# Issuing the stores of x's high part and of the partial output from ScalarE instead of SyncE

## The chip, the cores and the metric

The kernel runs on one core of a Trainium2 chip. The metric is the device time of one execution in microseconds (us). A core has TensorE (PE, matmuls), VectorE (DVE), ScalarE (ACT), GpSimd (POOL) and SyncE (SP); each runs its own instruction stream in order, and they wait for one another on semaphores. In the kernel before, every DMA is issued from SP's stream.

## The reference

Attention over 4 batches and 8 heads of 576 positions and 64 features, then a gated feed-forward block over the 2304 rows that it makes:

```python
scores = scale * np.matmul(q, k.transpose(0, 1, 3, 2))      # causal, softmax over keys
local = np.matmul(a, v)
mem_out = einsum(q_p, M_prev) / (einsum(q_p, z_prev) + 1e-6)  # q_p = phi(q)
x = g * mem_out + (1 - g) * local                            # rows: 2304 x 512
h = x @ w_in                                                 # 512 x 2048
g = h * np.tanh(np.log1p(np.exp(h)))
out = g @ w_out                                              # 2048 x 512
```

## The kernel before

**Attention.** Sixteen pairs of heads (`for p in range(NP)`) go through `scores` (matmuls, the row minimum on DVE at line 374, the exponential on ACT at line 381), `norm` (POOL at lines 87 and 93), `transp` (transposes, copied out of PSUM by DVE and ACT) and `av`. `av` leaves a pair's 128 columns of x as two parts: `xo`, the high part, cast by ACT out of PSUM (line 481, recorded at the helper's line 110), and `xl`, the rest, made by DVE behind it. `put` (line 484) stores both to the DRAM buffers `xs`: `xo` at line 486, `xl` at line 487. A pair has two casts to `xo`, 320 and 256 columns wide; the store follows the second.

**Feed-forward, first part.** Matmuls with w_in and w_out run on numbers split into high and low parts. The weights come as 512 KB pieces `raw` (line 152, two buffers), and `narrow` turns each into a high and a low part: `wa` on ACT (line 91), `ws` on DVE (line 156), joined on DVE (line 162), a mask on DVE (line 165), the last reading of `raw` on DVE (line 172, after which the buffer can be loaded again), the high part by ACT (line 110) and the low part by DVE (line 87). The first 6 of 16 columns of blocks (`KA`) are converted during attention, and while attention goes on `slot_a` multiplies blocks of 512 rows of x by them (line 233). `out_a` sums their share of the output in PSUM (`acc`, line 246), ACT copies it to the one buffer `ob` (line 251, recorded at line 110), and line 253 stores it to the DRAM buffer `part`. There are 18 such stores, one for each 128 rows.

**Feed-forward, second part.** `tail` first merges what is left of the first part with the conversion of seven more columns, then runs the other 10 columns over all rows (lines 566 and 583), reading x again from `xs` (line 205), and adds `part`, read back at line 581, before the output is stored at line 590.

**What sets the order.** The program is written as lists of steps; a scheduler with its own estimate of every instruction's time then orders each engine's stream, with priorities by stage (`OFF`). A stream is fixed before the run. Each DMA's completion is counted on one of eight semaphores, DMAHW0 to DMAHW7, that are handed out in turn over all DMAs; a DMA waits in its issuing stream until the one before it on the same semaphore has landed.

Of the kernel before, what the change touches and what calls it, by code (L numbers as in the profile page):

```python
# [49 lines left out]
def f32(ap):  # L50
    return ap.bitcast(F32)
# [25 lines left out]
def attention_moe_kernel(ctx: ExitStack, tc: tile.TileContext, f_src, qn, vn, zz, beta, w_in, w_out, out):  # L77
    nc = tc.nc
# [7 lines left out]
    def tt(name, **kw):  # L86
        engines[ENG[name]].tensor_tensor(**kw)  # L87
# [15 lines left out]
    def queued(ins, chain):  # L103
        if chain:
            order_after(ins, before[0])
        before[0] = ins

    def copy(which, o, i):
        if which == "a":
            nc.scalar.copy(out=o, in_=i)  # L110
        elif which == "v":
            nc.vector.tensor_copy(out=o, in_=i)  # L112
        else:
            nc.gpsimd.tensor_scalar(out=o, in0=i, scalar1=1.0, scalar2=1.0, op0=ALU.mult, op1=ALU.mult)
# [13 lines left out]
    xs = [dram.tile([128, 2, NC, S], F32, name=f"xs{b}") for b in range(B)]  # L128
    part = dram.tile([NT, DM], F32, name="part")
# [110 lines left out]
    def out_a(j, t):  # L240
        pool, tag = (("a", "acc"), ("h", "h"))[t % 2]
        acc = pool_of[pool].tile([128, DM], F32, tag=tag, name="acc")
        for f in range(KA):
            g = T[j, f]["g"]
            for y, z in ((0, 0), (1, 0), (0, 1)):
                nc.tensor.matmul(  # L246
                    acc[:], g[:, y, 128 * t:128 * t + 128], wo[z, f],
                    start=(f == 0 and y == z), stop=(f == KA - 1 and z == 1),
                )
        o = cp.tile([128, DM], F32, tag="ob", name="ob", bufs=1)  # L250
        copy("a", o[:], acc[:])
        r0 = BLOCKS[j][0] + 128 * t
        nc.sync.dma_start(out=part[r0:r0 + 128, :], in_=o[:])

    def steps_a(j):
        def first():
            X[j] = load_x(*BLOCKS[j])

        return ([first] + [lambda f=f: slot_a(j, f) for f in range(KA)]
                + [lambda t=t: out_a(j, t) for t in range(BLOCKS[j][1] // 128)])  # L260
# [3 lines left out]
    def attention():  # L264
# [194 lines left out]
        def av(p):  # L459
            d = pr[p]  # L460
            at = [hd[2 * p + e]["at"] for e in range(2)]

            def mms(j):
                if j == 0:
                    d["xo"] = tp.tile([128, S], F32R, tag="xo", name="xo", bufs=2)
                    d["xl"] = tp.tile([128, S], F32, tag="xl", name="xl", bufs=2)
                q0, ops = AVJ[j]
                n = ops[0][2]
                ps = g_["v", j] = ps_v.tile([128, n], F32, tag="v", name="vps")
                last = len(ops) - 1  # L470
                for k, (t, a, b, gi, c) in enumerate(ops):
                    for e in (1, 0):
                        queued(nc.tensor.matmul(  # L473
                            ps[64 * e:64 * e + 64, a:b], d["v"][:, t, e], at[e][gi][:, c:c + b - a],
                            start=(k == 0), stop=(k == last),
                        ), k or e == 0)

            def cp(j):
                q0, n = AVJ[j][0], AVJ[j][1][0][2]
                xo = d["xo"][:, q0:q0 + n]  # L480
                copy("a", xo, g_["v", j][:])
                tt("xlo", out=d["xl"][:, q0:q0 + n], in0=g_["v", j][:], in1=f32(xo), op=ALU.subtract)

            def put():
                b, c = divmod(p, 4)
                nc.sync.dma_start(out=xs[b][:, 0, c, :], in_=f32(d["xo"][:]))
                nc.sync.dma_start(out=xs[b][:, 1, c, :], in_=d["xl"][:])

            g_ = {}
            ops = []  # L490
            for j in range(2):
                ops += [lambda j=j: mms(j), lambda j=j: cp(j)]
            return ops + [put]
# [6 lines left out]
            out=mask[:, 448:576], in_=mask[:, 448:576], pattern=[[-1, 128]], compare_op=ALU.is_ge,  # L500
# [169 lines left out]
```

## Time and profile before

| | |
|---|---|
| median of 3 runs | 655.2 us (653.29 to 656.19) |
| the profiled execution's own time | 654.77 us |
| its span, first to last instruction | 653.0 us |
| PE, DVE, ACT, POOL busy | 597.0, 336.8, 300.7, 169.1 us |
| mean granted TensorE clock | 0.973 of full speed |
| DMA issues of line 486, 487, 253 | 16, 16, 18, all from SP |

Attention ends at about 336 us. From there to about 420 us the first part's rest and the weight conversion run together; from 420 us on PE works without pause. A busy time is a sum over the span and says nothing by itself about what is waited for; for that the waits, the chain of work that ended last and the stretches by stage are read.

### The profile page before, as it was taken

Reading aid. Unit: us, or ns where it says so; the run is one execution under the profiler, and the core shown is the slowest. Engines: PE = TensorE matmul, PEld = TensorE weight load, DVE = VectorE, ACT = ScalarE, POOL = GpSimd, SP = SyncE. Lnnn points to the kernel's source line nnn. Section 1 sums busy time; section 2 is a strip of 40 time slices with the busy share of each in tenths; the row PEclk is TensorE's granted clock in tenths of the full one; section 3 lists DMA queues with packets and bytes.
Section 4 is the critical chain, followed back from the end, with each engine's and each line's share of the span. In section 5 each row is a group of like instructions: output and inputs, shape, how many; then the busy total and the mean of one; then the engine's idle time right before and its main releaser. Section 6 shows DMA issues by size and latency. Waiting matters only on the chain.

```text
span 653.0 us, 9308 instructions
## 1 busy us (share of the span) xinstructions
PE 597.0 (91%) x3200; PEld 454.9 (70%) x3200; DVE 336.8 (52%) x903; ACT 300.7 (46%) x694; POOL 169.1 (26%) x260
## 2 busy tenths in 40 slices
PE   3477968889989999999998979999999999999997
PEld 2254635656655766767776878888888888888886
DVE  4989897765588654573338887920311211121121
ACT  3677655866567675566325455621222222222221
POOL 3697886464166714443000000000000000000000
PEclk9979986899999999999999989999999999999999
DMA  6345674324275226421257765304302220430220
GB/s 229 104 144 182 189 262 150 133 61 144 76 235 168 98 62 176 166 73 58 91 176 235 261 206 176 121 1 129 130 0 82 94 83 6 124 129 0 65 97 33
DMA packets 47007, 80.83 MB, mean 124 GB/s; under 512 B 7280, under 2 KB 21616, under 8 KB 46960
## 3 DMA queue, kind: packets, MB, share of 16 engines
q1 hardware_dynamic: 46960, 80.24, 38.0%
q8 instruction: 25, 0.41, 0.3%
q14 instruction: 22, 0.18, 0.1%
HBM read 61.35 MB, written 18.87 MB: 123 GB/s over the span
## 4 chain that ended last, share of the span: by engine, by line
PE 61%; DVE 13%; DMA 10%; ACT 7%; POOL 5%; issue 2%; SPq 1%; DVEq 0%; ACTq 0%; POOLq 0%
PE o L583 19%; PE h L566 19%; PE acc L246 7%; PE h L233 5%; DMA raw<-in_w_in_dram 5%; PE vps L473 5%; PE t L445 4%; DVE w L374 3%; PE s L364 3%; POOL w L93 3%; DMA raw<-in_w_out_dram 3%; DMA qn<-in_qn_dram 2%; ACT w L381 2%; ACT L217 1%; DVE ws L172 1%
## 5 line engine op out<-in xcount | busy, mean ns | idle before, releaser
L87 DVE TENSOR_TENSOR g<-u,g 128x512 fp32r<-128x512 f32 (+1 forms) x80 | 52.4, 661 | 185.6 <-ACT g L110 185.6
L566 PE MATMUL h<-xb,wi 128*128 128x512 f32 (+1 forms) x600 | 134.9, 368 | 0.0
L583 PE MATMUL o<-wo,g 128*128 128x512 f32 x540 | 133.8, 390 | 0.0
L217 ACT ACTIVATE u<-h 128x512 f32<-128x512 f32 (+1 forms) x80 | 43.5, 554 | 179.2 <-PE h L566 170.9
L566 PEld LDWEIGHTS h<-xb,wi 128*128 128x128 f32 x600 | 106.1, 188 | 19.6
L583 PEld LDWEIGHTS o<-wo,g 128*128 128x128 f32 x540 | 100.6, 188 | 20.3
L93 POOL TENSOR_SCALAR w<-w,rc 128x64 f32<-128x64 f32 (+4 forms) x160 | 95.4, 621 | 71.0 <-ACT w L381 53.3
L381 ACT ACTIVATE w<-w,mx 128x576 f32<-128x576 f32 (+4 forms) x160 | 88.3, 554 | 28.5 <-DVE mx L374 27.6
L364 PE MATMUL s<-f 64*128 64x288 f32 (+4 forms) x384 | 69.2, 472 | 31.7 <-DVE mx L374 25.4
L233 PE MATMUL h<-xb,wi 128*128 128x512 f32 (+1 forms) x360 | 88.0, 389 | 7.8 <-ACT u L217 7.8
L246 PE MATMUL acc<-wo,g 128*128 128x512 f32 x324 | 85.9, 401 | 1.4 <-ACT ob L110 0.9
L445 PE MATMUL t<-ident,w 128*128 128x128 f32 x480 | 75.5, 291 | 5.3 <-ACT at L110 3.1
L233 PEld LDWEIGHTS h<-xb,wi 128*128 128x128 f32 x360 | 64.8, 200 | 21.1 <-ACT u L217 9.6
L364 PEld LDWEIGHTS s<-f 64*128 64x128 f32 x384 | 35.4, 207 | 59.0 <-DVE mx L374 33.2
L445 PEld LDWEIGHTS t<-ident,w 128*128 128x128 f32 x480 | 55.9, 146 | 26.0 <-issue 8.7
L246 PEld LDWEIGHTS acc<-wo,g 128*128 128x128 f32 x324 | 59.4, 190 | 16.0 <-issue 2.3
L374 DVE CUSTOM_DVE_ANT_0 w<-s,mask 128x288 f32<-128x288 f32 (+4 forms) x160 | 59.6, 421 | 17.6 <-PE s L364 17.6
L473 PE MATMUL vps<-at,v 128*64 128x256 f32 (+2 forms) x512 | 61.3, 383 | 5.8 <-DVE xl L87 3.7
L473 PEld LDWEIGHTS vps<-at,v 128*64 128x64 f32 x512 | 35.6, 142 | 31.7 <-issue 6.0
L112 DVE COPY at<-t 128x448 f32<-128x448 f32 x64 | 41.5, 649 | 16.2 <-PE t L445 16.2
L110 ACT CAST g<-u 128x512 fp32r<-128x512 f32 (+1 forms) x80 | 45.5, 579 | 1.8
L110 ACT COPY at<-t 128x384 f32<-128x384 f32 x64 | 33.7, 526 | 17.6 <-PE t L445 17.4
(45 smaller groups left out, 432.1 us busy)
## 6 DMA issues: line engine op xcount, KB each, us to landing
f<-in_f_src_dram SPq DMA_DIRECT2D x32, 288.0 KB, 3.7
raw<-in_w_in_dram SPq DMA_DIRECT2D x16, 512.0 KB, 3.9
raw<-in_w_out_dram SPq DMA_DIRECT2D x16, 512.0 KB, 3.5
xb<-xs SPq DMA_DIRECT2D x24, 256.0 KB, 3.7
qn<-in_qn_dram SPq DMA_DIRECT2D x16, 320.0 KB, 3.4
v<-in_vn_dram SPq DMA_DIRECT2D x16, 320.0 KB, 3.3
xs<-xo SPq DMA_DIRECT2D x16, 288.0 KB, 3.4
xs<-xl SPq DMA_DIRECT2D x16, 288.0 KB, 3.3
```

What stands on the lines that cost most here:

```text
L87: engines[ENG[name]].tensor_tensor(**kw)
L93: engines[which].tensor_scalar(out=o, in0=i, scalar1=scale, scalar2=1.0, op0=ALU.mult, op1=ALU.mult)
L110: nc.scalar.copy(out=o, in_=i)
L233: ins = nc.tensor.matmul(ps, wi[y, f][:, c, :], x[c][:, z], start=(q == 0), stop=(q == 11))
L246: nc.tensor.matmul(acc[:], g[:, y, 128 * t:128 * t + 128], wo[z, f], start=(f == 0 and y == z), stop=(f == KA - 1 and z == 1),)
L364: nc.tensor.matmul(g["ps"][:, o:o + n], f[le, 0, q0:q0 + 128], f[le, 1, a:b], start=True, stop=True)
L374: nc.vector.tensor_tensor_reduce(out=g["w"][:, WO[m] + D + a:WO[m] + D + b], in0=g["ps"][:, o:o + n], in1=mask[:, c0:c0 + n], scale=-E_SC, ...
L381: nc.scalar.activation(out=row, in_=row, func=ACTF.Exp, scale=-1.0, bias=g["mx"][:, m:m + 1], accum_out=g["sm"][:, m:m + 1])
L445: nc.tensor.transpose(ps[:, o:o + 128], g["w"][:, c:c + 128], ident[:])
L473: queued(nc.tensor.matmul(ps[64 * e:64 * e + 64, a:b], d["v"][:, t, e], at[e][gi][:, c:c + b - a], start=(k == 0), stop=(k == last),), k o ...
L566: nc.tensor.matmul(ps[:, :n], wi[a, f][:, c, :], x[c][:, b], start=(k == 0), stop=(k == 11))
L583: nc.tensor.matmul(D_[t][:], g[:, y, 128 * t:128 * t + 128], wo[z, f], start=(f == KA and y == z), stop=(f == NF - 1 and z == 1),)
```

## The change

Two issues move from SP's stream to ACT's, the store of `xo` and the store of `ob`. The store of `xl` stays on SP, and so do all loads and the output. The scheduler makes its order anew.

```diff
         copy("a", o[:], acc[:])
         r0 = BLOCKS[j][0] + 128 * t
-        nc.sync.dma_start(out=part[r0:r0 + 128, :], in_=o[:])
+        nc.scalar.dma_start(out=part[r0:r0 + 128, :], in_=o[:])
...
                 b, c = divmod(p, 4)
-                nc.sync.dma_start(out=xs[b][:, 0, c, :], in_=f32(d["xo"][:]))
+                nc.scalar.dma_start(out=xs[b][:, 0, c, :], in_=f32(d["xo"][:]))
                 nc.sync.dma_start(out=xs[b][:, 1, c, :], in_=d["xl"][:])
```

ACT gains 34 rows and loses none; its 17 changes of activation table after the first stand in the same sequence. POOL's order is the same, and up to the end of attention SP's differs by the rows taken out, PE's not at all, and ACT's and DVE's by a few swaps of neighbours. From the end of attention on there are more swaps.

On ACT in the middle of attention, this is what stands now, with the semaphores that each row waits for (numbers behind names tell buffers apart; `phe` is the exponential of `prep`):

```order
L253 DMA part_77<-ob_1736 128x512 [waits DMAHW7_49,Activation_49]
L110 COPY at_1461<-t_1462 128x512 [waits PE_49]
L110 COPY ob_1758<-acc_1739 128x512 [waits DMAHW7_49]
L253 DMA part_77<-ob_1758 128x512 [waits DMAHW1_49,Activation_49]
L318 ACTIVATE phe_2238<-phe_2238 128x640 [waits DVE_49,Pool_49]
```

The two DMA rows are new in this stream; each waits for ACT's own copy and for an earlier DMA's semaphore.

On SP at the end of attention (about 336 to 344 us before), the difference; `raw` are weight pieces, `xb` blocks of x, `pp` the partial output read back:

```order
 L152 DMA raw<-in_w_in_dram 128x1024
-L486 DMA xs_76<-xo 128x576
+L152 DMA raw<-in_w_out_dram 128x1024
 L487 DMA xs_76<-xl 128x576
-L152 DMA raw<-in_w_out_dram 128x1024
 L205 DMA xb<-xs_76 128x320
-L253 DMA part<-ob 128x512
+L152 DMA raw<-in_w_in_dram 128x1024
 L205 DMA xb<-xs_76 128x320
-L581 DMA pp<-part 128x512
-L152 DMA raw<-in_w_in_dram 128x1024
-L581 DMA pp<-part 128x512 x3
```

Two weight loads have moved ahead: the second in front of the store of `xl`, the third in front of an x block and of the four `pp` loads.

On DVE in the conversion (about 357 to 361 us before), before the change:

```order
L165 TENSOR_SCALAR ws_3717<-wa_3716 128x512
L87 TENSOR_TENSOR wo1_7_3457<-wa_3666,ws_3667 128x512
L172 SCALAR_TENSOR_TENSOR ws_3717<-raw_3715,ws_3717 128x512
L87 TENSOR_TENSOR wa_3716<-wa_3716,wi0_8_3461 128x512
L87 TENSOR_TENSOR g_3757<-u_3756,g_3757 128x512
L156 TENSOR_SCALAR ws_3765<-raw_3763 128x512
```

And now:

```order
L87 TENSOR_TENSOR wo1_7_3457<-wa_3666,ws_3667 128x512
L165 TENSOR_SCALAR ws_3717<-wa_3716 128x512
L156 TENSOR_SCALAR ws_3765<-raw_3763 128x512
L172 SCALAR_TENSOR_TENSOR ws_3717<-raw_3715,ws_3717 128x512
L87 TENSOR_TENSOR wa_3716<-wa_3716,wi0_8_3461 128x512
L87 TENSOR_TENSOR g_3757<-u_3756,g_3757 128x512
```

Line 156 on the next piece, which waits for that piece to land, has moved in front of line 172 on the piece at hand, which frees the other `raw` buffer. The same has happened one column further on (`raw_3863` in front of the release of `raw_3811`).

On ACT at about 381 to 387 us before, the difference; `u` is the activation of the first 256 rows wide block:

```order
 L110 CAST wi_11_3482<-wa 128x512
 L110 COPY ob<-acc 128x512
 L91 ACTIVATE wa<-raw 128x512
-L217 ACTIVATE u<-h 128x256
-L110 CAST g<-u 128x256
-L110 COPY ob<-acc 128x512
+L253 DMA part<-ob 128x512
+L217 ACTIVATE u<-h 128x256
+L110 CAST g<-u 128x256
 L110 CAST wo_11_3483<-wa 128x512
```

A store now stands between `wa` and `u`, and the second copy to `ob` comes later.

## Rows read from the trace of the kernel before

**Rows 1.** The page: busy time of each engine; shares of the chain that ended last.

```profile
PE 597.0 (91%) x3200; PEld 454.9 (70%) x3200; DVE 336.8 (52%) x903; ACT 300.7 (46%) x694; POOL 169.1 (26%) x260
...
PE 61%; DVE 13%; DMA 10%; ACT 7%; POOL 5%; issue 2%; SPq 1%; DVEq 0%; ACTq 0%; POOLq 0%
```

**Rows 2.** Stretches: length, busy time (instructions) by engine, PE clock, DMA share, GB/s.

```profile
47.00:160.00 113.00, 94.52 (x573) 62.66 (x571) 90.33 (x268) 75.51 (x186) 73.28 (x97) 0.91 0.52 165
160.00:335.70 175.70, 169.97 (x1086) 120.14 (x1085) 97.27 (x323) 102.65 (x263) 66.53 (x119) 1.00 0.37 118
335.70:386.35 50.65, 44.46 (x197) 35.88 (x197) 40.61 (x74) 25.44 (x45) 0.00 (x0) 0.99 0.74 243
386.35:420.00 33.65, 33.65 (x165) 29.46 (x166) 27.66 (x55) 18.85 (x37) 0.00 (x0) 0.91 0.52 177
420.00:653.00 233.00, 229.10 (x1067) 191.69 (x1065) 45.49 (x74) 52.26 (x95) 0.00 (x0) 1.00 0.21 68
```

**Rows 3.** SP's waits, whole span: line, releaser, us in total, times, longest.

```profile
SPq L152 <- DVE ws L172: 59.5, 23, 7.3
...
SPq L253 <- ACT ob L110: 40.7, 16, 8.7
SPq L486 <- ACT xo L110: 33.1, 7, 23.1
...
SPq L487 <- DVE xl L87: 7.4, 5, 2.4
```

**Rows 4.** The chain that ended last, 342 to 387 us: start, length, what.

```profile
342.09 6.16 DMA raw<-in_w_in_dram
...
359.56 3.95 DMA raw<-in_w_in_dram
...
368.61 6.44 DMA raw<-in_w_in_dram
...
382.08 3.19 DMA raw<-in_w_out_dram
...
385.35 0.68 ACT wa L91
386.03 0.28 ACT u L217
...
386.35 2.93 PE h L233 x12
```

**Rows 5.** PE's waits from 335.7 to 420 us.

```profile
PE h L233 <- ACT u L217: 5.3, 3, 3.3
```

**Rows 6.** Issues of the two stores: ns shortest/median/longest, first and last start.

```profile
L486 SPq DMA_DIRECT2D xs<-xo x16: 319/354/413, 53.6 to 336.2; - x16
...
L253 SPq DMA_DIRECT2D part<-ob x18: 319/320/1172, 161.8 to 410.0; - x18
```

**Rows 7.** Timeline of SP, 341 to 358 us: start, length, line, what.

```profile
341.54 0.42 SPq L581 DMA_DIRECT2D pp<-part  x1
342.09 0.37 SPq L152 DMA_DIRECT2D raw<-in_w_in_dram  x1
...
351.60 5.31 SPq L253 DMA_DIRECT2D part<-ob  x2
357.34 0.33 SPq L152 DMA_DIRECT2D raw<-in_w_out_dram  x1
```

**Rows 8.** Timeline of ACT: start, length, line, what [idle before, releaser].

```profile
153.66 0.35 ACT L110 CAST xo<-vps 128x256 fp32r<-128x256 f32 x1
...
154.90 0.56 ACT L381 ACTIVATE w<-w,mx 128x320 f32<-128x320 f32 x1 [0.36 <-DVE mx L374]
...
166.49 0.74 ACT L318 ACTIVATE phe<-phe 128x640 f32<-128x640 f32 x1 [1.46 <-DVE phe L313]
```

**Rows 9.** Timeline of DVE, 356 to 361 us.

```profile
356.10 0.69 DVE L172 SCALAR_TENSOR_TENSOR ws<-raw,ws 128x512 f32<-128x512 uint32 x1
...
360.88 0.43 DVE L156 TENSOR_SCALAR ws<-raw 128x512 int32<-128x512 int32 x1
```

## The prediction

> **What bounds the kernel now.** I read the shares of the chain first: PE holds 61% of it, DVE 13%, DMA 10%, ACT 7%, and SP's own stream 1% [rows 1]. So time that SP spends issuing stores is hardly ever what the end waits for, and time that ACT spends issuing them falls on an engine with a small share. Then I split the span by stage [rows 2]. From 47 to 160 us PE is busy for 94.5 of 113.0 us, and DVE (90.3), ACT (75.5) and POOL (73.3) share what is waited for. From 160 to 335.7 PE is busy for 170.0 of 175.7: at most 5.7 us can be won. From 335.7 to 386.35 it is busy for 44.5 of 50.65, so 6.2 us are idle; PE waited 5.3 us there for `u` from ACT, once for 3.3 us [rows 5], and the chain runs through weight loads, DVE's conversion and ACT's `wa` up to 386.35, where PE takes it over [rows 4]. From 386.35 to 420 PE never pauses, at a granted clock of 0.91, and from 420 on it is busy for 229.1 of 233.0 at full clock [rows 2]. The change issues its last store at 410.0 [rows 6], so what it does must be done before 420.
>
> SP's waits come next [rows 3]. They look large: 40.7 us at line 253 for ACT's copy and 33.1 at line 486 for ACT's cast. Taking them away frees only what stands behind them, and that must be looked up case by case.
>
> **Part 1: SP loses 34 issues.** At medians of 0.354 and 0.320 us [rows 6] that is 16 x 0.354 + 18 x 0.320 = 11.4 us of SP's stream. Behind line 486 nearly always stands line 487, which waits for `xl`, made by DVE after `xo`; it keeps 7.4 us of waits of its own [rows 3] and will take over most of the 33.1. Behind line 253 stand loads that wait for their buffers: weight loads wait 59.5 us for DVE's line 172 [rows 3]. Going through the 18 stores I found one load that a store held: the pair of stores from 351.60 ends at 356.91, and the weight load behind it goes out at 357.34, though line 172 had freed its buffer at 356.79 (356.10 + 0.69) [rows 7, 9]. That is 0.5 us, beside the chain, which takes the load of 359.56. Part 1 by itself: 0.
>
> **Part 2: ACT gains 34 issues.** No row shows a DMA issued by ACT. From below the price is 0, if the issue fits under the running instruction; from above I take SP's longest issue of line 253, 1.17 us [rows 6]. I take 0.35 us, SP's medians, plus 0.1 where the store directly follows its copy and the next instruction can't overlap with it: the same kind of instruction should take as long in another stream. So ACT spends some 34 x 0.4 = 14 us more.
>
> By stage: 23 stores lie before 335.7, 9 between 335.7 and 386.35, 2 after. For each of the 23 I looked up ACT's next idle time behind it. In 17 it is 0.7 us or more, as at 166.49, where ACT sits idle for 1.46 us behind a copy to `ob` [rows 8]; these hide the issue. In 6 it is 0.34 to 0.58 us, as at 154.90 [rows 8], and in one of these two stores share one gap of 0.35. What sticks out is about 0.1 x 6 + 0.35 = 1 us of ACT; PE, busy for 97% of the stretch from 160 on, waits for ACT in few of these places. I take +0.4 us; the bounds are 0 and, at 1.17 us an issue, some 7 us sticking out, of which half on the path: +3.5.
>
> Of the 9, eight stand beside ACT's idle time while it waits for weights. The ninth stands between `wa` and `u`, where the chain passes: 385.35, 386.03, then PE at 386.35 [rows 4]. All of its 0.35 us lands there. The last 2 lie beside PE's unbroken work: 0. Part 2: +0.75 us, from 0 to +5.
>
> A store on ACT also waits for an earlier DMA's semaphore. If that DMA were still unissued in SP's stream, ACT would stand with it. I compared each store's moment with the DMA eight places earlier in the order: nearly all were issued 4 us or more before and had landed. Cost 0.
>
> **Part 3: the new order from 336 us on.** Here the loads run close together: 243 GB/s against 118 in the stretch before [rows 2]. The third weight load, issued at 342.09 behind a `pp` load, took 6.16 us; others on the chain took 3.2 to 3.95 [rows 4, 7]. With the x block and `pp` behind it instead of in front, I work out a landing about 1.6 us earlier: 416 KB less ahead at roughly 260 GB/s. The conversion then starts its next column 1.4 us earlier. But the next piece, loaded behind the four `pp`, lands when it did. Two columns later DVE's new order costs: line 156 waits for the next piece before line 172 frees the other buffer. Stepping DVE's rows through with its own durations (0.43, 0.60 to 0.70 and 0.44 us) and 3.5 to 3.95 us a load, the release that leads to the load of 359.56 comes 0.2 us later than before, that of 368.61 comes 0.8 us later, and that of 382.08 comes 1.1 us earlier, since there the new order frees first. So `wa` before 386.35 starts 1.1 us earlier: -1.1. The bounds: PE becomes the limit and the whole 6.2 us idle goes [rows 2], or the loads at the two new waiting places take 6.2 to 6.4 us, as those of 342.09 and 368.61 did [rows 4], which is 2 x 2.7 = +5.4.
>
> **The sum.** 0 + 0.75 - 1.1 = -0.35 us on the profiled execution's 654.77, its span of 653.0 and 1.8 around it: 654.4. That execution lies 0.4 under the median of 655.2, so for a median I forecast 654.8: no change that a measurement of this kernel, which tells apart about 0.5% or 3.3 us, can show.
>
> **The rivals.**
>
> *Faster: the conversion stops being the limit.* With stores on another stream, loads go out as soon as their buffers are free, and the stage from 335.7 loses most of its 6.2 us of PE idle time, some with it of the clock, which fell from full 2.4 GHz to a mean of 0.91 (1.2 GHz for part of the stretch) behind the pause before 386.35 [rows 2]; at 0.09 of 33.65 us that is up to 3 us more. I price it at 4 to 7 us: 648 to 651, say 650. For it: weight loads are on the chain seven times here, and the new order puts two ahead. Against it: only one load was held by a store, and the loads wait for line 172. The Trainium skill, Perfetto Trace Analysis, section DMA Optimizations, advises to give inputs to one issuing engine and outputs to another so that they spread more freely. By that rule this rival would be the forecast, at 650; no run here shows it yet, and SP's rows speak for a small effect, since what waits behind the stores waits for buffers.
>
> *Slower: DVE waits for a load before it frees the buffer for the next.* This is the upper bound of part 3. At two places more than before the two `raw` buffers work one after the other. While loads land in under about 4.5 us the gains elsewhere cover it; at 6 us or more the stage grows by up to 5.4 us, and since PE has no work of its own ahead, the end does too: 654.8 + 1.1 + 5.4 = 661; in the middle 659.5. For it: two loads of that stage took over 6 us. Against it: the x blocks and `pp` that slowed them have moved.
>
> *Slower: ACT is held at its stores.* At 0.8 us or more an issue the idle behind 10 or so of the 23 is used up, the stores beside `wa` in the conversion stick out too, and I get +4 to +5: 659. The Trainium skill, Perfetto Trace Analysis, section DMA Instruction — HWDGE (DVE, Sync), speaks for this: it says that a DMA's semaphore wait, its wait for the descriptor generator's lock and the issue all take place in the issuing engine's sequencer. By it an ACT store behind its own copy stops what follows until the copy is written; my 0.1 us stands for that, and a wait for the lock would come on top. No row here can show the lock.
>
> *That the stores don't leave SP* is excluded: SP's order has lost exactly those rows.
>
> **How the numbers follow.** Forecast, within noise: 0.62. Faster rival: 0.18. DVE's order: 0.12; ACT held: 0.08. Faster by over 0.5% is under 651.9, slower over 658.5, so the chances are 0.18, 0.62 and 0.20. For 8 in 10 the range takes in half of each side: down to 650.5, and up to 660.0.
>
> **What would show it.** Issues of lines 486 and 253 in ACT's stream of 0.3 to 0.4 us; SP's waits at line 487 grown to nearly the 33 us of line 486; the weight load near 342 landing in under 5 us; PE's wait for `u` near 386 shortened to 2 to 3 us; from 420 on the same pace. I am wrong about ACT if its issues take over 0.8 us or POOL and PE wait longer for line 381; about DVE if line 156 stands idle for a load for over 2 us at the two new places; about SP if weight loads go out well before they did although line 172 runs when it did.

## The result and the profile after

The changed kernel takes 659.17 us (median; 657.1 to 661.56) against 655.69 us for the kernel before on the same chip: a ratio of 1.0051, 95% interval 1.0036 to 1.0065. It is slower by about 3.5 us. The time lies in the predicted range (650.5 to 660.0), but "no change that can be measured" was wrong.

The profiled execution of the changed kernel took 660.73 us, its span is 658.9. One execution is a coarse measure here: the traces of the experiments below include a second one of each kernel, and the two of before have spans of 653.0 and 658.5. So sizes are taken from the timed ratios, and the traces are read for what is waited for.

The stretches of [rows 2], in the kernel after (length, busy time of PE, PEld, DVE, ACT, POOL with instructions, PE clock, DMA share, GB/s):

```profile
160.00:335.70 175.70, 170.28 (x1064) 120.18 (x1063) 96.97 (x323) 102.74 (x263) 67.40 (x120) 0.98 0.37 119
335.70:386.35 50.65, 46.44 (x210) 36.20 (x209) 35.94 (x65) 22.62 (x40) 0.00 (x0) 1.00 0.67 220
386.35:420.00 33.65, 28.47 (x153) 25.09 (x152) 27.69 (x54) 17.01 (x35) 0.00 (x0) 0.95 0.61 193
420.00:653.00 233.00, 233.00 (x1086) 195.18 (x1085) 48.81 (x81) 56.65 (x103) 0.00 (x0) 1.00 0.22 69
```

From 386.35 to 420 PE no longer works without pause: 28.47 us of 33.65, where before it was 33.65. In the last stretch PE is busy throughout; the 229.10 us of before mean only that its program ends inside the stretch. In this trace the last cast of attention also starts 3.0 us later than before (338.71 against 335.71 us), which is taken up with C2 below. Behind it, the conversion of the weights, up to 420 us, is where to look.

The new issues on ACT, which answer to [rows 6] (ns shortest/median/longest, first and last start), and then the SP waits that answer to [rows 3] (line, releaser, us in total, times, longest):

```profile
L253 ACTq DMA_DIRECT2D part<-ob x18: 326/326/353, 162.2 to 414.8; - x18
...
L486 ACTq DMA_DIRECT2D xs<-xo x16: 326/326/360, 53.9 to 339.1; - x16
```

```profile
SPq L152 <- DVE ws L172: 88.9, 27, 8.0
...
SPq L487 <- DVE xl L87: 50.9, 13, 23.7
```

An issue costs ACT 326 ns, and line 487 has taken over line 486's waits. Both are as predicted. The surprise is in the chain that ended last, 379 to 393 us (start, length, what), which answers to [rows 4]:

```profile
381.48 0.58 ACT ob L110
382.05 0.03 ACT wa L91
382.08 3.10 DMA part<-ob
...
385.26 0.07 ACT ob L110
385.33 0.42 issue
385.75 0.14 ACT wo L110
385.88 5.66 DMA part<-ob
...
391.62 0.07 ACT ob L110
391.69 0.41 issue
392.10 0.46 ACT wa L91
...
392.66 0.38 ACT u L217
...
393.09 2.08 PE h L233 x8
```

Two stores of the partial output stand on the chain, for 3.10 and 5.66 us. `ob` is one buffer: ACT's next copy to it waits until the store before has landed, and as ACT works in order, `wa` and `u` behind that copy wait too. PE gets `u` at 393.09, which is 54.4 us behind the last cast; before, at 386.35, 50.6 us behind it. Of what ACT and PE waited for between 335 and 425 us, these rows count:

```profile
ACT ob L110 <- DMA part<-ob: 7.5, 4, 2.6
...
PE h L233 <- ACT u L217: 6.9, 2, 5.2
```

In the trace of before ACT waited 0.5 us, once, for a part store there, and PE's longest wait for `u` was 3.3 us [rows 5]:

```profile
ACT ob L110 <- DMA part<-ob: 0.5, 1, 0.5
```

One trace is little: in the second trace of before these are 3.3 us and 4.5 us.

Why do the stores land so late? SP's weight loads after, and then SP's stream before with the same two loads and the same two stores (start, us, line, what):

```profile
382.18 0.33 SPq L152 DMA_DIRECT2D raw<-in_w_in_dram  x1
385.51 0.33 SPq L152 DMA_DIRECT2D raw<-in_w_out_dram  x1
```

```profile
376.25 0.32 SPq L253 DMA_DIRECT2D part<-ob  x1
377.69 0.33 SPq L152 DMA_DIRECT2D raw<-in_w_in_dram  x1
379.00 0.32 SPq L253 DMA_DIRECT2D part<-ob  x1
382.08 0.33 SPq L152 DMA_DIRECT2D raw<-in_w_out_dram  x1
```

Before, each 256 KB store stood ahead of a 512 KB load in one stream. After, the loads no longer stand behind the stores: the first store (382.08) goes out 0.10 us ahead of its load, the second (385.88) 0.37 us behind the load that it used to precede. Before, the second store left 1.30 us behind the first load and took 4.04 us to land; but ACT's next copy to `ob` came only at 383.81, when it had landed.

### The profile page after: what moved, and what is told of

Read it like the earlier page. It is cut to its first block, busy times and chain, and to the rows that moved or that the text cites. A ratio compares the mean times of both kernels' runs of the same rounds, so it can differ in the third digit from the quotient of the medians.

```text
span 658.9 us, 9294 instructions
## 1 busy us (share of the span) xinstructions
PE 598.8 (91%) x3200; PEld 455.1 (69%) x3200; DVE 335.9 (51%) x903; ACT 300.8 (46%) x694; POOL 169.2 (26%) x260
## 4 chain that ended last, share of the span: by engine, by line
PE 63%; DVE 11%; DMA 10%; ACT 7%; POOL 6%; issue 2%; SPq 1%; DVEq 0%; ACTq 0%; POOLq 0%
PE o L583 19%; PE h L566 18%; PE acc L246 7%; PE vps L473 5%; PE h L233 5%; PE t L445 4%; PE s L364 4%; POOL w L93 4%; DMA raw<-in_w_out_dram 4%; DMA raw<-in_w_in_dram 3%; DVE w L374 3%; ACT w L381 2%; DMA qn<-in_qn_dram 2%; DMA part<-ob 1%; POOL w L87 1%
```

## The experiments

The theories: **A**, the single buffer `ob` by itself; **B**, the new order of PE, DVE and the loads from 336 us on; **C**, ACT's issues in the attention; **C2**, one store in the attention, that of the seventh pair at 177 us, behind which PE pauses and its clock falls; **D**, the new order and the late part stores on ACT cost together, and neither does alone; **E**, many small delays. Ratios are to the kernel before on the same chip, with a 95% interval.

### One half of the change each

**e1: line 253 alone on ACT.**

```diff
-        nc.sync.dma_start(out=part[r0:r0 + 128, :], in_=o[:])
+        nc.scalar.dma_start(out=part[r0:r0 + 128, :], in_=o[:])
```

> The kernel before with only the stores of the partial output (line 253) on ScalarE; the cast's stores (line 486) stay on SyncE. Theory A (the single buffer ob: an ACT-issued store starts later or lands later, ACT stands at the next copy to ob and keeps wa and u behind it): slower than before by most of the 3.5 us, 2 to 4 us; ACT's waits for a part store grow from 4.8 us in all to 8 or more, most of it between 336 and 425 us. Theory B (the new order of DVE and the loads from 336 us on, which the moved cast stores bring about): as before, within 1 us, and ACT's waits for part stores stay near 5 us. Theory C (the price of the issues on ACT in the attention, seen as the 2 to 3 us that after lost between 184 and 207 us): half of that, +1 to +1.5 us.

Measured: 0.9975 (0.9958 to 0.9992), a little faster. ACT's waits for part stores are 9.0 us in all, 4.6 of them between 335 and 425 (before: 4.8 and 0.5, in its second trace 7.7 and 3.3). So these waits grew and nothing was lost: A alone falls, and the issues of these 18 stores on ACT (C) cost nothing.

**e2: line 486 alone on ACT.**

```diff
-                nc.sync.dma_start(out=xs[b][:, 0, c, :], in_=f32(d["xo"][:]))
+                nc.scalar.dma_start(out=xs[b][:, 0, c, :], in_=f32(d["xo"][:]))
```

> The kernel before with only the stores of x's high part (line 486) on ScalarE; the partial output's stores (line 253) stay on SyncE. PE's order is then that of after, DVE's nearly. Theory A (single buffer ob): within 1 us of before, ACT's waits for part stores near 5 us. Theory B (the new order from 336 us on): as slow as after, +3 to +4 us, though ob is stored as in before. Theory C (issue cost in the attention): +1 to +1.5 us, all of it before 336 us.

Measured: 1.0035 (1.0011 to 1.0058), between B and C. In its trace PE also pauses for 2.72 us near 190 us, which led to C2.

**e3 and e4: two buffers for `ob`**, e3 in the changed kernel, e4 in the kernel before.

```diff
-        o = cp.tile([128, DM], F32, tag="ob", name="ob", bufs=1)
+        o = cp.tile([128, DM], F32, tag="ob", name="ob", bufs=2)
```

> The changed kernel with two buffers for ob in place of one (line 250). Theory A: the copy no longer waits for the store before it, ACT's waits for part stores go to about 0 and the 3 to 4 us come back: about the time of before, 655 to 656 us. Theory B: the order from 336 us on stays unfavourable, 658 to 660 us. The order of the program also shifts with the second buffer, so that the number of waits decides beside the time.

> The kernel before with two buffers for ob. Theory A: only the 4.8 us of ACT's waits for part stores can go, of which about 1 us lies in the conversion: 0 to 1 us faster than before, so that the gain of the second buffer in the changed kernel is 3 us larger than here. Theory B: the second buffer gains as little or as much in both kernels.

Measured: e3 0.9981 (0.9965 to 0.9997), e4 0.9924 (0.9897 to 0.9952). The second buffer takes 0.7 to 0.8% off both, where A expected it to be worth 3 us more in the changed one. e4 is the fastest kernel of this study, 653.41 us. The second buffer also changes the order of all engines, so it doesn't tell what of its gain is the buffer.

### Single stores

The scheduler's order turned out to hang on one store: with the part stores on SP, PE's and DVE's order from 336 us on is the new one when the last pair's high part is stored by ACT, and before's when it is not, whatever the other fifteen do; with the part stores on ACT it is the new one or that of e1, which is close to before's. That lets order and stores be set apart. In the edits `p` is the pair, from 0.

```diff
-                nc.sync.dma_start(out=xs[b][:, 0, c, :], in_=f32(d["xo"][:]))
+                (nc.scalar if p == 15 else nc.sync).dma_start(out=xs[b][:, 0, c, :], in_=f32(d["xo"][:]))
```

This is e5; e6 has `p != 15` and e7 `p == 6`. e8 and e9 are the changed kernel with `p not in (6, 15)` and `p != 15`.

> The kernel before with one store moved to ScalarE, that of the sixteenth and last pair's high part (near 336 us). Every other store stays on SyncE, yet PE's and DVE's order from 336 us on is that of the kernel with all sixteen moved. Theory B (the order): as before until 336 us, within 0.5 us there, then 2 to 3 us lost between 336 and 420 us; about +2 to +3 us in all. Rival C2 (the store of the seventh pair at 177 us lands later from ScalarE's ring, PE pauses near 192 us and its clock falls): nothing lost, within 0.5 us of before.

> The complement: fifteen of the high part's sixteen stores on ScalarE, the last one on SyncE; PE's and DVE's order is that of before throughout. Theory B: nothing is lost behind 336 us. Rival C2: 2 to 3 us are lost near 185 to 205 us, with the granted clock under 1.00 there, and the total is +2 to +3 us. If both hold, e5 and e6 each lose about half of what the kernel with all sixteen loses in its profiled run (5.3 us).

> The kernel before with one store moved to ScalarE, that of the seventh pair's high part (near 177 us). PE's and DVE's order is that of before. Rival C2: that store alone lands a microsecond or more later than 3.9 us, the x-block load that reads it back waits 2.4 us or more for it (0.8 before), PE pauses over 1.9 us between 188 and 196 us, the granted clock falls there, and the time is +2 to +3 us. Theory B: as before, within 0.5 us.

> The changed kernel with two of its 34 moved stores put back on SyncE, those of the seventh and the sixteenth pair's high part. If the loss sits in these two places (C2 and B together), the other 32 moved stores cost nothing: within 1 us of before or up to 1.6 us faster, as the run with the partial output's stores alone on ScalarE was. If the loss is the issue price of all 34 on ScalarE, it stays at +3 us.

Measured: e5 1.0001 (0.9981 to 1.0020), e6 1.0013 (0.9994 to 1.0032), e7 1.0010 (0.9989 to 1.0031), e8 0.9993 (0.9967 to 1.0018). B gave e5 2 to 3 us, and C2 gave as much to e6 and e7. By the ends of the intervals e5 costs 1.3 us at most, e6 and e7 some 2 us at most, and all three perhaps nothing. e8 says that the loss does sit with these two stores, or one of them. C2's mechanism is in the trace of e7 all the same; here PE's pause (start, us, what, idle before), and then the 5 us in which it lies (columns as in the stretches above):

```profile
192.06 3.59 PE L473 MATMUL vps<-at,v 128*64 128x256 f32 x20 [2.48 <-DVE xl L87]
```

```profile
190.00:195.00 5.00, 2.94 (x14) 1.71 (x16) 3.89 (x13) 3.42 (x12) 0.81 (x1) 0.66 0.42 149
```

In before the pause was 1.09 us and the same matmuls took 2.17 us at full clock. The x-block load that reads the store back waits 2.4 us for it (0.8 in before), a part store stands behind that load in SP's stream, the next copy to `ob` behind the store, and the load of `qn`, for which DVE and then PE wait, behind the second part store. In the timing that is at most 2 us (the interval's end) and perhaps nothing: the second trace of before lost 1.2 us there as well, without a fall of the clock.

> The changed kernel with one of its 34 moved stores put back on SyncE, that of the last pair's high part; PE's order is then that of the run with the partial output's stores alone. Theory C2 (the seventh pair's store) says that 2 to 3 us are still lost between 177 and 207 us and the granted clock falls near 195; theory B says that nothing is lost from 336 to 420 us. Both together: 1 to 2 us faster than after, +1 to +2.5 us against before.

> The changed kernel once more, beside a second trace of before on the same chip. If the two places of loss belong to the kernel and not to one execution, this trace shows them again: the pause and a granted clock under 0.9 between 190 and 205 us (+2 to +3 us against before), and the ScalarE copy held behind a part store near 381 to 393 us (+2 to +3 us). If they were chance, one of them is missing. Time: 0.3 to 0.65% over before.

> The kernel before as one of the kernels compared, for a second trace of it on a chip whose runs are to be compared. Theories B and C2: granted clock 1.00 between 190 and 205 us, PE taking over from ScalarE's u near 386 us after a wait of 3 to 4 us, total within 0.2% of before. If the trace of before was a lucky execution, one of the two losses shows here too, and the loss put down to the change is smaller.

Measured together on one chip: e9 0.9994 (0.9972 to 1.0016), the changed kernel again (e10) 1.0060 (1.0040 to 1.0080), the kernel before against itself (e11) 1.0009 (0.9989 to 1.0028). One store of 34 put back takes all of the loss away, and it is the one that sets the order. The trace of e11 tells how far to trust a trace: with before's own order it lost 3.7 us behind 336 us against the first trace of before (span less the start of the last cast to `xo`: 321.0 against 317.3 us). The changed kernel's two traces have 320.2 and 321.6 us there, and PE gets `u` 54.4 and 55.6 us behind the last cast, in e11 also 54.4. So by such lengths single traces of the two kernels can't be told apart. What comes back in both traces of the changed kernel, and not in either of before, is the two part stores on the chain; in e10:

```profile
379.49 3.35 DMA part<-ob
...
383.54 5.45 DMA part<-ob
```

The fall of the clock came back too (granted 0.80 in 190 to 195 us; in the first trace 0.51 in 195 to 200), but not C2's pause: in both traces of the changed kernel PE stands still there for 0.83 us at a time at most. Against the first trace of before, the way from the seventh to the ninth pair's cast is 1.0 us longer in e10, not 2.9 as in the first trace of the changed kernel.

### The two causes, together and apart

What stayed open was why the last store matters in the changed kernel and costs nothing alone. D says: because the ten part stores behind it are on ACT too. e13 is e5 with this edit, e15 the kernel before with it, and e14 the changed kernel with those ten stores back on SP (`j` is the block of 512 rows).

```diff
-        nc.sync.dma_start(out=part[r0:r0 + 128, :], in_=o[:])
+        (nc.scalar if j >= 2 else nc.sync).dma_start(out=part[r0:r0 + 128, :], in_=o[:])
```

> The kernel before with eleven stores on ScalarE: that of the last pair's high part (which brings the new order of PE and DVE from 336 us on) and the ten stores of the partial output behind it. Theory D (the two parts of the change cost only together: in the new order, a part store from ScalarE holds the next copy to ob, and with it wa and u): nearly the whole loss of the changed kernel, +2 to +4 us; ScalarE's waits for part stores between 335 and 425 us 7 us or more, PE busy there for 81.5 us or less of 90. Theory E (no single place; the loss is the small delays of all 34 issues in the attention): within 1 us of before.

> The changed kernel with the ten partial-output stores behind 336 us put back on SyncE; the other 24 moved stores stay on ScalarE, PE's and DVE's order is exactly that of after. Theory D: most of the loss goes, 0 to +1.5 us against before; ScalarE's waits for part stores between 335 and 425 us 6 us or less. Theory E: still +2.5 us or more. Theory B alone (the order is enough): still +2.5 us or more.

> The kernel before with only the ten partial-output stores behind 336 us on ScalarE, in the order of the run with all 18 there. Theory D: not slower, between 0.996 and 1.001 of before, PE busy for 83 us or more of the 90 between 335 and 425 us, as in the three traces with this order and these stores on ScalarE. If part stores on ScalarE cost in any order: +2 us.

Measured, with the others that share a cell:

| order from 336 us on | late part stores on SP | late part stores on ACT |
|---|---|---|
| as before, or nearly | before against itself (e11) 1.0009; e6 1.0013; e7 1.0010 | e15 **0.9972** (0.9955 to 0.9988); e1 0.9975; e8 0.9993; e9 0.9994 |
| new | e5 **1.0001** (0.9981 to 1.0020); e14 **1.0009** (0.9985 to 1.0033); e2 1.0035 (1.0011 to 1.0058) | e13 **1.0044** (1.0027 to 1.0061); after 1.0051; e10 1.0060 |

e13 moves eleven stores and has most of the loss of all 34. It differs from e5 in the issuer of ten stores alone, since PE's, DVE's and ACT's own orders are identical; the intervals of the two don't meet. e14 differs from the changed kernel in the same ten stores and is level with before; its interval doesn't meet those of after and e10. So D holds; B alone, A alone and E don't. The entry that fits badly is e2: it stands in a cell that should cost nothing. With it the mean of that cell is 1.0015, against 1.0052 in the cell with both causes. Two of the numbers that D named missed: ACT's waits in e14 are 6.5 us (6 or less), and PE is busy for 82.41 us in e15 (83 or more).

The traces bear this out in part. From the last matmul of attention (line 473) to the first of line 583, PE has the same 336 matmuls in every kernel here. This stretch (columns as above), in this sequence: before, e5, e15, e13, after:

```profile
335.66:414.04 78.38, 72.19 (x336) 60.44 (x336) 63.13 (x118) 39.61 (x72) 0.00 (x0) 0.96 0.67 223
```

```profile
335.12:417.31 82.19, 74.56 (x337) 61.02 (x336) 62.59 (x117) 39.48 (x72) 0.00 (x0) 0.94 0.66 211
```

```profile
334.83:413.69 78.86, 71.27 (x335) 59.19 (x336) 62.79 (x118) 39.17 (x72) 0.00 (x0) 0.98 0.68 220
```

```profile
336.14:418.45 82.31, 72.47 (x336) 59.30 (x336) 62.76 (x117) 39.68 (x72) 0.00 (x0) 0.96 0.67 210
```

```profile
338.66:419.63 80.97, 71.58 (x336) 59.17 (x336) 63.29 (x118) 39.34 (x72) 0.00 (x0) 0.98 0.67 216
```

Length less busy time is PE's idle time: 8.9 to 9.8 us in the three traces with both causes (after, e10, e13), 6.2 to 8.4 in the eleven others with one `ob`. PE's longest wait for `u` is 5.2 to 5.4 us in the three and 2.7 to 4.5 in the others; here e5 and then e13, from 335 to 425 us:

```profile
PE h L233 <- ACT u L217: 4.3, 2, 3.2
```

```profile
PE h L233 <- ACT u L217: 7.1, 3, 5.4
```

The length itself doesn't bear it out. It is 81.0 to 82.4 us in the three, but 80.6 to 82.2 in the traces with the new order and the late stores on SP (e2, e5, e14; the granted clock was 0.94 in two of them), and 76.8 to 82.1 with the order of before or nearly. Read by length, the traces would rather speak for B. That the two causes cost only together rests on the timed ratios, and the traces don't account for the size of the loss. e13's chain carries the pair of part stores:

```profile
380.15 3.51 DMA part<-ob
...
384.36 5.53 DMA part<-ob
```

None of the other traces with one `ob` has a part store on the chain between 360 and 400 us. And this is the mechanism side by side; first e5, the new order with the stores on SP, where store and load stand in one stream, and ACT's copies to `ob` between them:

```profile
380.77 0.32 SPq L253 DMA_DIRECT2D part<-ob  x1
381.20 0.37 SPq L152 DMA_DIRECT2D raw<-in_w_in_dram  x1
...
383.73 0.32 SPq L253 DMA_DIRECT2D part<-ob  x1
384.16 0.37 SPq L152 DMA_DIRECT2D raw<-in_w_out_dram  x1
```

```profile
383.12 0.59 ACT L110 COPY ob<-acc 128x512 f32<-128x512 f32 x1 [1.79 <-DMA part<-ob]
387.07 0.58 ACT L110 COPY ob<-acc 128x512 f32<-128x512 f32 x1
```

Both times the store leaves first and lands in some 2.2 us (the copy of 383.12 waited for the first), and the second copy doesn't wait. In e13 the same pair goes out from two streams:

```profile
380.25 0.33 SPq L152 DMA_DIRECT2D raw<-in_w_in_dram  x1
383.57 0.33 SPq L152 DMA_DIRECT2D raw<-in_w_out_dram  x1
```

```profile
383.74 0.59 ACT L110 COPY ob<-acc 128x512 f32<-128x512 f32 x1 [3.04 <-DMA part<-ob]
384.36 0.33 ACTq L253 DMA_DIRECT2D part<-ob  x1
...
389.96 0.58 ACT L110 COPY ob<-acc 128x512 f32<-128x512 f32 x1 [2.20 <-DMA part<-ob]
```

The load of 383.57 no longer stands behind the store, leaves 0.79 us ahead of it, and the store takes 5.53 us.

The load isn't all that was in its way. In e13, from the store's issue to its landing (384.36 to 389.89 us), first the busy share of the DMA engines in 40 slices, then a queue:

```profile
DMA  0999763497859898989999610000101000000000
q8 instruction: 1, 0.02, 1.1%
```

Of the store's 128 packets of 2 KB, 120 had ended after 3.36 us. The last eight came one behind another and took 1.69 us more; the first of them started as a 16 KB packet of q8, a queue that the profile calls instruction, ended. The same stands in the two traces of the changed kernel: 3.69 and then 1.49 us in the first, 3.96 and 1.02 in e10. Other stores of these three traces that left 0.55 to 0.61 us behind a load, without such a packet, took 3.68 to 4.30 us. What the packet costs in time, no run separates; in e5 it came at 385.60 beside a load, which took 4.61 us.

In e15, with nearly before's order, the two stores shown leave ACT 1.5 and 0.6 us ahead of the load that follows, and the copy behind each is not held:

```profile
376.31 0.33 ACTq L253 DMA_DIRECT2D part<-ob  x1
...
378.44 0.59 ACT L110 COPY ob<-acc 128x512 f32<-128x512 f32 x1
...
384.86 0.33 ACTq L253 DMA_DIRECT2D part<-ob  x1
...
387.48 0.58 ACT L110 COPY ob<-acc 128x512 f32<-128x512 f32 x1
```

The store between them, at 379.06, left 1.26 us behind a load and took 4.59 us, but the next copy came only at 384.25 and wasn't held either.

So ACT's queue isn't slow in itself; a store is slow in it behind a weight load. It is so in SP's stream too: the store of 412.74 in e5 left 0.62 us behind a load and took 4.39 us. In the new order with the stores on ACT, the store comes behind the load, and the next copy comes before it has landed. The Trainium skill, DMA: Bandwidth & Descriptors, section Issuing engines are not separate DMA queues, says that transfers started by different engines end up on the same 16 DMA engines and interleave. That agrees with the 3.68 to 5.66 us behind a load and the at most 2.1 us (376.31 to 378.44) ahead of one; no run here shows how the engines choose between the two queues.

**e12: a kernel meant to beat both**, e1 with two buffers for `ob`.

> A kernel meant to beat both: the partial output's stores on ScalarE, the high part's stores on SyncE, and two buffers for ob. The two single steps gave 0.9975 and 0.9924 of before. If they add, 0.990; if the gain of both is the same one (the copy to ob no longer waits), 0.992 to 0.994.

Measured: 0.9947 (0.9928 to 0.9967), 654.3 us. It beats the kernel before and the changed one, but the gains don't add: e4, with all stores on SP, is at least as good.

## Why the prediction was wrong, point by point

**Where it could act.** Right: from 420 on PE works without pause at full clock as before, 233.00 of 233.00 us.

**Part 1, SP.** The takeover by line 487 was right (50.9 us, of which 7.4 were its own before). "0 on the path" looked only for loads that would gain by going out earlier, and found 0.5 us. It didn't ask what an earlier load does to the store that it used to stand behind. That is half of the step that failed.

**Part 2, ACT.** The price of an issue was right, 0.326 us for 0.35, and the waits for earlier DMAs' semaphores cost nothing that shows (the one wait of ACT for a part store that isn't before a copy to `ob`, 1.9 us at 164.10, was as long before the change, for PE). The step that failed is "Of the 9, eight stand beside ACT's idle time while it waits for weights", counted as 0. It priced the issue and left out the landing: ACT's next copy to the one buffer `ob` waits for it. These waits went from 0.5 us (3.3 in the second trace of before) to 7.5 between 335 and 425 us (8.6 in e10). Their sum alone is no loss, as e14 has 6.5 and e1 4.6; the two of 2.63 and 2.33 us at 385.26 and 391.62 are on the chain. They were not idle time that was there anyway, since `wa` and `u` stand behind the copy in ACT's stream. The working had line 253's waits for `ob` from SP's side [rows 3], and the order showed a store between `wa` and `u`; the landing times of the stores, and who waits for them, don't enter the sum.

**Part 3, the order.** The forecast was -1.1 us. Order alone (e5) is between -1.2 and +1.3 us by its interval, so this term isn't refuted, but its signs failed: the third weight load took 5.43 us (issued at 345.59; under 5 was forecast), and PE's wait for `u` was 5.2 us at its longest, not 2 to 3. What the step missed is the order on ACT: with the new one, the copies to `ob` come in a place where the store of one lies beside a weight load. e5 and e13 show that the new order costs only with these stores on ACT.

**The rival "DVE waits for a load".** Not the cause: line 156's waits for w_out pieces rose from 1.4 to 3.6 us after, but to 6.9 us in e5, which lost nothing that the timing shows. Its price "in the middle", 659.5, isn't worked out: the middle between the forecast of 654.8 and 661 is 657.9.

**The rival "ACT is held at its stores".** It gave 659, the time that came, and the right engine; but its mechanism was a dear issue or the lock, and the issue took 0.326 us. ACT was held at the copy behind the store, so that the number agrees is luck.

**The rival "faster".** By the Trainium skill's advice in Perfetto Trace Analysis, section DMA Optimizations, inputs and outputs from two engines spread more freely. Here that freedom is the loss in the new order (e13, 1.0044), while e15, 0.9972, is what it may bring in another; e15's order isn't quite before's, so the 0.3% isn't shown to be the queue's.

**What stays open.** e2, all high-part stores without the part stores, is at 1.0035 (1.0011 to 1.0058), more than e5 and e6 add up to (0.0001 + 0.0013), though its interval reaches down to 1.0011. e14 has all sixteen of e2's stores on ACT and eight more, and is at 1.0009, so chance may be a part of it. The early stores may cost up to 2 us; no run separated that from noise. Open too is how the loss divides between the load ahead of the store and the q8 packet.

## What to carry to other kernels

A store in the same stream as the loads behind it has a right of way over them: moved to another engine's queue, it starts no earlier than its copy, while loads that stood behind it can now start before it. When a store is moved, price its landing and who waits for its buffer, not its issue; with one buffer the wait comes back on the very engine that now issues it, and everything behind it in that stream is late. Look at the two effects of an edit together: here the new order and the new issuer of the late stores each cost nothing that could be measured (but for the open e2), and both together 0.4 to 0.6%.

## What the runs showed of the hardware that was not expected

A 256 KB store that left 0.55 to 0.61 us behind a 512 KB load from the other issuing engine took 3.68 to 4.30 us to land (seven stores in after, e10, e13). Three that left 0.37 to 0.79 us behind one took 5.45 to 5.66; there the last eight of 128 packets followed a 16 KB packet of the queue that the profile calls instruction. Those that left 0.10 us ahead of a load took 3.10 to 3.51; with the load 1.5 us behind it the store had landed within 2.1 (e15).

The length of the last pause didn't decide whether PE's clock fell. Behind 2.48 us without work near 192 us the mean granted clock of 190 to 195 us was 0.66 and a group of matmuls took 3.59 us, where at the full 2.4 GHz it takes 2.17 (e7): part of it ran at 1.2 GHz. In the second trace of before, behind 2.16 us without work at the same place, the clock stayed at 1.00. Behind pauses of 0.83 and 0.57 us it fell in both traces of the changed kernel (to a mean of 0.51 in 195 to 200 us in the first), and behind pauses of the same lengths in e14 it stayed at 1.00.
